# Key-value products of the first block moved behind their chunk's output products, in a linear-attention and mixture-of-experts kernel

## The chip, the cores and the metric

The kernel runs on one core of one Trainium2 chip. The metric is device time in microseconds (us) of one execution, as a median over runs.

## The reference

Three layers follow one another. The first is a linear attention with decay: for each batch and head a state of 48 x 48 is decayed by `w` and gains the outer product of key and value at each of 768 positions; the output at a position is the receptance vector times the state, plus a term of the position itself weighted by `u`. The second is a dense layer pair, the third a mixture of 8 experts, top 2.

```python
for t in range(S):
    kt, vt, rt = (k[:, :, t], v[:, :, t], r[:, :, t])
    cur = np.einsum('bhd,bhe->bhde', u[None] * kt, vt)
    y[:, :, t] = np.einsum('bhd,bhde->bhe', rt, state + cur)
    state = w[None, :, :, None] * state + np.einsum('bhd,bhe->bhde', kt, vt)
...
h = x @ w_in
r = np.maximum(h, 0.0)
g = r * r
return (g @ w_out).astype(np.float32)
```

Sizes: 4 batches, 8 heads, 768 positions, head dimension 48; 3072 tokens of 384; dense width 2048; expert width 1024.

## The kernel before, in words

**Chunks.** The attention is cut into chunks of 128 positions, numbered q = 0 to 23, six to a batch (`CPB`). A chunk with all its heads gives 128 tokens of 384. The steps of a chunk:

- `pre`, `pre_k`, `pre2` (lines 386 to 424): elementwise products of receptance and keys on GpSimd, a reduction on VectorE (line 414), diagonal blocks of the score tile `am` on ScalarE (line 419).
- `p_tr` (line 426): transposes of receptance (`r`) and keys (`k`) on TensorE into one bank each (line 439), then a multiply on VectorE (line 444) or a copy on ScalarE (line 448) out of it.
- `p_a` (line 454): scores, 16 matmuls into two banks (line 459), then two masked copies on VectorE into `am` (line 463).
- `p_y` (line 467): the output in one bank. Part 0 multiplies the state `Z` (24 matmuls, none in the first chunk of a batch), part 1 the scores and values (32 matmuls), all on line 477. Behind part 1 stands `load(q + 2, "v")` (line 491): the values have two buffers, so chunk q + 2 takes that of chunk q.
- `p_kv` (line 494): the key-value product, 32 matmuls into one bank (line 503), then two VectorE operations that take it out into the next state (line 510, or 513 in the first chunk of a batch) and, except in the first chunk, two multiplies on GpSimd (line 511). In the last chunk of a batch it returns at once (line 496).
- `p_x` (line 515): the output is split into a high part on ScalarE (line 522) and a low part on VectorE (line 523), which are the input of the dense layer.

**Banks.** Outside the opening list, `p_tr`, `p_a`, `p_y` and `p_kv` all draw their PSUM bank by `bank()` with the tag "att" (line 171), which has three banks. A bank is given back, in the order of the program, behind the last instruction that uses it.

**Blocks and slots.** The dense layers run over six blocks of 512 tokens (four chunks each). In block j, 16 steps f alternate `mm1` (line 532, nine matmuls into hidden columns, line 540), `gsplit` (ReLU and square, lines 545 to 555), and `mm2` of two steps earlier (line 558, lines 565 and 571). Behind `mm1` of step f stands slot 2f, behind `mm2` slot 2f + 1. Into these slots the table `CHUNKS` (line 36) puts the chunk steps of the next block: one row for each of four chunks, nine times in the order pre, p_tr r, p_tr k, pre2, p_kv, p_a, p_y part 0, p_y part 1, p_x. The whole part of a number is the slot, the fraction the place in it. So in block 0 the chunks 4, 5, 6 and 7 are placed. Chunks 0 to 3, and the first steps of chunk 4, stand in the opening list `HEAD` (line 27).

**Conversion.** In block 0 the dense weights, pieces 0 to 15, are converted beside the matmuls: `conv_w1` (line 270) on ScalarE (line 272), `conv_w2` (line 274) four steps on VectorE (lines 279, 280, 281 and 288 or 291), `conv_w3` (line 294) on ScalarE (line 301) and GpSimd (line 302). Their slots stand in `CONV_AT`. `conv_w2` of piece 5 is in slot 4, that of piece 13 in slot 21.

**Order.** The schedule is by hand: each engine does its instructions in the order in which the program issues them.

Of the kernel before, what the change touches and what calls it, by code (L numbers as in the profile page):

```python
# [34 lines left out]

CHUNKS = (((0.72, 2.09, 0.63, 0.83, 1.23, 3.2, 1.96, 5.12, 6.53),
# [56 lines left out]
def body(ctx, tc, r, k, v, w, u, w_in, w_out, w_gate, w_noise, noise, w1, w2, out):  # L93
# [11 lines left out]
    CPB = S // P  # L105
# [65 lines left out]
    def bank(tag="att", bufs=3):  # L171
        return ps.tile([P, 512], F32, name=tag, tag=tag, bufs=bufs)
# [11 lines left out]
    def load(q, names="rkv"):  # L184
        if q >= NCH:
            return
        b, c = divmod(q, CPB)
        for nm in names:
            if nm in L.get(q, {}):
                continue  # L190
            if nm == "r" and q < QD:
                t = rp[q % 2][:, :, :D]
            elif nm == "r":
                t = at.tile([P, H, D], F32, name="lr", tag="s3", bufs=1)
            elif nm == "k" and q == 0:
                t = kp[0][:, :, :D]
            elif nm == "v":
                t = at.tile([P, H, D], F32, name="lv", bufs=2)
            else:
                t = at.tile([P, H, D], F32, name="l" + nm, bufs=2)  # L200
            nc.sync.dma_start(t, SRC[nm][b, :, c * P:(c + 1) * P, :].rearrange("h s d -> s h d"))
            L.setdefault(q, {})[nm] = t
# [178 lines left out]
                          C["zero2"][:, None, :].to_broadcast([P, b - a, DM]))  # L381

    x1h, x1l = {}, {}
    A = {}

    def pre(q):
        a = A.setdefault(q, {})
        l = L[q]
        if q:
            pre_k(q)  # L390
        if q < QD:
            t = at.tile([P, H, D], F32, name="ra", bufs=2)
        else:
            t = at.tile([P, H, D], F32, name="rk", bufs=1)
        nc.gpsimd.tensor_mul(t, l["r"], l["k"])
        nc.gpsimd.tensor_mul(t, t, ub)
        a["rk"] = t
        load(q + 2, "k")

    def pairs(q):  # L400
        return L[q]["v"].rearrange("p (a s) d -> p a (s d)", s=2)
# [8 lines left out]
    def pre2(q):  # L410
        a, l = A[q], L[q]
        t = a["rk"]
        dg = at.tile([P, H], F32, name="dg", bufs=2)
        nc.vector.tensor_reduce(dg, t, axis=AX.X, op=OP.add)

        a["am"] = at.tile([P, H, P], F32, name="am", tag="am", bufs=2)
        if q < OWN_ACT:
            for h in range(H):
                nc.scalar.activation(a["am"][:, h, :], ident, AF.Copy, scale=dg[:, h:h + 1])
        else:  # L420
            nc.gpsimd.tensor_mul(a["am"], ident[:, None, :].to_broadcast([P, H, P]),
                                 dg[:, :, None].to_broadcast([P, H, P]))

        nc.gpsimd.tensor_copy(ends(q), pairs(q)[:, :, 32:64].rearrange("p a (s x) -> p a s x", s=2))

    def p_tr(q, which, *tag):
        a = A.setdefault(q, {})
        if q >= QD:
            t = a[which + "T"] = at.tile([P, HP, P], F32, name=which + "T", bufs=2)
            nc.vector.transpose(t.rearrange("p a (s i) -> p a i s", i=TQ),  # L430
                                turned[which].rearrange("p a (i x) -> p a i x", x=D)[:, :, :, :32])
            nc.gpsimd.tensor_mul(t[:KR], t[:KR], T[:KR] if which == "r" else T[:KR, :, ::-1])
            if which == "k":
                load_next(q + 1)
            return
        src = (rp if which == "r" else kp)[q % 2]
        pb = bank(*tag)
        for hp in range(HP):
            nc.tensor.transpose(pb[:KR, hp * P:(hp + 1) * P],
                                src.rearrange("p h x -> p (h x)")[:, hp * P:hp * P + KR], ident)  # L440
        t = at.tile([P, HP, P], F32, name=which + "T", bufs=2)
        src = pb[:KR].rearrange("p (h t) -> p h t", t=P)
        if which == "r":
            nc.vector.tensor_mul(t[:KR], src, T[:KR])
        elif q == 0:
            nc.vector.tensor_mul(t[:KR], src, T[:KR, :, ::-1])
        else:
            nc.scalar.activation(t[:KR], src, AF.Copy)
        if which == ("r" if q == TPB else "k"):
            if q + 2 < QD:  # L450
                load(q + 2, "r")
        a[which + "T"] = t

    def p_a(q, *tag):
        a = A[q]
        pbs = [bank(*tag), bank(*tag)]
        for hp in range(HP):
            for j in range(2):
                nc.tensor.matmul(pbs[j][:, hp * P:(hp + 1) * P], a["kT"][64 * j:64 * j + D, hp, :],  # L459
                                 a["rT"][64 * j:64 * j + D, hp, :], start=True, stop=True)  # L460
        am = a["am"].rearrange("p (h j) t -> p h j t", j=2)
        for j in range(2):
            nc.vector.copy_predicated(am[:, :, j, :], mask.bitcast(mybir.dt.uint16)[:, None, :].to_broadcast([P, HP, P]),  # L463
                                      pbs[j].rearrange("p (h t) -> p h t", t=P))

    def p_y(q, part):
        a = A[q]
        c = q % CPB  # L470
        if part == 0:
            a["y"] = bank()
        pb = a["y"][:, :DM].rearrange("p (d t) -> p d t", t=P)

        def add(g, x, y, **kw):
            d, n = divmod(g, 4)
            nc.tensor.matmul(pb[32 * n:32 * n + 32, d, :], x, y, skip_group_check=True, **kw)  # L477

        if part == 0:
            for g in range(KD * 4 if c else 0):  # L480
                hp, s = divmod(g, 3)
                add(g, Z[c % 2][:KR, hp, 32 * s:32 * s + 32], a["rT"][:KR, hp, :], start=(g < 4), stop=False)
            return
        v, am = pairs(q), a["am"].rearrange("p (a s) t -> p a s t", s=2)
        for g in range(KD * 4):
            hp, s = divmod(g, 3)
            add(g, vx[q % 2][:, hp, 0, :] if s == 1 else v[:, hp, 32 * s:32 * s + 32], am[:, hp, s // 2, :],
                start=(g < 4 and c == 0), stop=(s != 1))
        for hp in range(HP):
            add(3 * hp + 1, vx[q % 2][:, hp, 1, :], am[:, hp, 1, :], start=False, stop=True)  # L490
        load(q + 2, "v")


    def p_kv(q, *tag):
        c = q % CPB
        if c == CPB - 1:
            return
        pb = bank(*tag)[:, :HP * D].rearrange("p (a d) -> p a d", d=D)
        kf = kp[q % 2].rearrange("p h x -> p (h x)")
        v = L[q]["v"]  # L500
        for hp in range(HP):
            for g in range(4):
                nc.tensor.matmul(pb[32 * g:32 * g + 32, hp, :], kf[:, hp * P + 32 * g:hp * P + 32 * g + 32],  # L503
                                 v[:, 2 * hp + g // 2, :], start=(hp == 0), stop=(hp == HP - 1), skip_group_check=True)
        for s in range(2):
            rows = slice(64 * s, 64 * s + D)
            zn = Z[(c + 1) % 2][rows, :, s * D:(s + 1) * D]
            w_ = wmid[rows, :, None].to_broadcast([D, HP, D])
            if c:
                nc.vector.tensor_add(zn, pb[rows], Z[c % 2][rows, :, s * D:(s + 1) * D])  # L510
                nc.gpsimd.tensor_mul(zn, zn, w_)
            else:
                nc.vector.tensor_mul(zn, pb[rows], w_)

    def p_x(q, *tag):
        j, i = divmod(q, TPB)
        if i == 0:
            x1h[j] = m1.tile([P, KD, BLK], F32R, name="x1h", bufs=2)
            x1l[j] = m1.tile([P, KD, BLK], F32R, name="x1l", bufs=2)
        src = A[q]["y"][:, :DM].rearrange("p (d t) -> p d t", t=P)  # L520
        hi = x1h[j][:, :, i * P:(i + 1) * P]
        nc.scalar.activation(hi, src, AF.Copy)
        nc.vector.tensor_tensor(x1l[j][:, :, i * P:(i + 1) * P], src, hi.bitcast(F32), op=OP.subtract)
        if q + 1 == QD:
            load_next(QD)
        del A[q], L[q]
# [536 lines left out]
    for j in range(NB):  # L1063
# [6 lines left out]
        if j + 1 < NB:  # L1070
            for i, at_ in enumerate(CHUNKS[min(j, 2)]):
                q = (j + 1) * TPB + i
# [194 lines left out]
```

## Time and profile before

| | us |
|---|---|
| median of 3 runs | 951.79 |
| lowest, highest | 951.40, 951.82 |
| profiled execution | 954.92 |
| span of the profiled execution, first to last instruction | 953.1 |
| busy TensorE in it | 938.8 |

The profile is that of one execution. Its span is what the rows below count in, from 0 to 953.1 us; the remaining 1.8 us lie around it. TensorE's mean granted clock was 0.998 of full speed.

### The profile page before, as it was taken

What the parts mean: (1) busy time and instruction counts of PE and PEld (TensorE: products, weight loads), DVE (VectorE), ACT (ScalarE), POOL (GpSimd) and SP (SyncE); (2) the same over time, 40 slices, a digit from 0 to 9 for tenths busy, and PEclk for the clock granted to TensorE, in tenths of its full rate; (3) what the DMA queues carried; (4) which work ended last, traced back from release to release, by engine and by line L of the source; (5) the groups of instructions that cost most, each with busy time, mean ns of one, the idle gap of its engine ahead of it and who ended that gap; (6) DMA issues with size and microseconds to landing.
All of it is one profiled execution on the core that took longest, in us unless ns stands there. A gap on an engine that the chain in (4) does not pass through costs nothing.

```text
span 953.1 us, 17746 instructions
## 1 busy us (share of the span) xinstructions
PE 938.8 (98%) x6845; PEld 805.3 (84%) x6845; DVE 540.4 (57%) x982; ACT 432.9 (45%) x792; POOL 349.2 (37%) x406
## 2 busy tenths in 40 slices
PE   8899999999999999999999999999999999999997
PEld 7677787778778878877888899999999898989987
DVE  8999756636845663684254564554545555356420
ACT  5666655334434444443555542443444444444321
POOL 6665353544573354455030344122121221212112
PEclk9999999999999999999999999999999999999999
DMA  7655379932432464442024367466545565545212
GB/s 179 165 163 165 96 191 302 244 108 64 94 104 56 111 153 122 111 99 86 1 100 93 108 134 188 104 135 135 130 97 115 120 121 109 114 92 109 36 21 37
DMA packets 193233, 112.32 MB, mean 118 GB/s; under 512 B 131777, under 2 KB 185698, under 8 KB 193122
## 3 DMA queue, kind: packets, MB, share of 16 engines
q1 hardware_dynamic: 181698, 91.03, 37.7%
q0 software_dynamic: 10624, 19.74, 11.3%
q8 instruction: 75, 1.23, 0.5%
q14 instruction: 36, 0.29, 0.1%
q10 hardware_dynamic: 800, 0.02, 0.0%
HBM read 74.64 MB, written 36.12 MB: 116 GB/s over the span
## 4 chain that ended last, share of the span: by engine, by line
PE 90%; DVE 5%; issue 1%; POOL 1%; ACT 1%; DMA 1%; POOLq 0%; DVEq 0%; ACTq 0%
PE ph L540 20%; PE xo L571 19%; PE ph L861 19%; PE y L918 14%; PE y L949 4%; PE att L477 3%; PE ph L949 2%; PE att L459 2%; PE att L604 2%; PE y L861 2%; PE xo L565 1%; PE att L962 1%; PE att L503 1%; DVE am L463 1%; DVE t L279 1%
## 5 line engine op out<-in xcount | busy, mean ns | idle before, releaser
L929 POOL DMA_INDIRECT out<-yt,id x56 | 87.1, 1556 | 298.1 <-ACT yt L927 257.4
L555 DVE TENSOR_TENSOR gl<-g,gh 128x512 fp32r<-128x512 f32 x90 | 77.2, 857 | 127.3 <-ACT gh L553 124.2
L904 DVE SCALAR_TENSOR_TENSOR hl<-ph,hh 128x512 fp32r<-128x512 f32 (+1 forms) x112 | 66.9, 599 | 113.1 <-ACT hh L903 109.2
L545 ACT ACTIVATE rt<-ph 128x512 f32<-128x512 f32 x96 | 57.1, 595 | 150.9 <-PE ph L540 146.4
L540 PE MATMUL ph<-x1h,wih 128*128 128x512 f32 x288 | 119.4, 414 | 0.0
L861 PE MATMUL ph<-xh,w0h 128*128 128x512 f32 (+3 forms) x336 | 118.1, 352 | 0.0
L861 PE MATMUL ph<-xl,w0h 128*128 128x512 f32 (+3 forms) x336 | 116.3, 346 | 0.2 <-DVE xl L830 0.2
L861 PE MATMUL ph<-xh,w0l 128*128 128x512 f32 (+3 forms) x336 | 116.1, 346 | 0.0
L540 PE MATMUL ph<-x1h,wil 128*128 128x512 f32 x288 | 112.4, 390 | 0.0
L540 PE MATMUL ph<-x1l,wih 128*128 128x512 f32 x288 | 112.3, 391 | 0.0
L571 PE MATMUL xo<-gh,wol 128*128 128x512 f32 x270 | 105.9, 392 | 0.0
L903 ACT ACTIVATE hh<-ph 128x512 fp32r<-128x512 f32 (+1 forms) x112 | 58.6, 524 | 88.9 <-PE ph L861 84.0
L918 PE MATMUL y<-w1h,hh 128*128 128x384 f32 x256 | 85.7, 335 | 0.0
L918 PE MATMUL y<-w1l,hh 128*128 128x384 f32 x256 | 85.6, 335 | 0.0
L918 PE MATMUL y<-w1h,hl 128*128 128x384 f32 x256 | 85.6, 334 | 0.0
L732 POOL DMA_INDIRECT sent<-row,si x48 | 50.3, 1049 | 61.4 <-DVE gl L555 45.0
L571 PE MATMUL xo<-gh,woh 128*128 128x512 f32 x180 | 71.6, 398 | 0.0
L571 PE MATMUL xo<-gl,woh 128*128 128x512 f32 x180 | 70.1, 390 | 0.0
L861 PEld LDWEIGHTS ph<-xl,w0h 128*128 128x128 f32 x336 | 63.3, 188 | 8.0 <-DVE xl L830 1.3
L861 PEld LDWEIGHTS ph<-xh,w0l 128*128 128x128 f32 x336 | 63.2, 188 | 7.7
L861 PEld LDWEIGHTS ph<-xh,w0h 128*128 128x128 f32 x336 | 63.3, 188 | 6.9 <-ACT xh L829 0.3
L540 PEld LDWEIGHTS ph<-x1h,wih 128*128 128x128 f32 x288 | 54.0, 188 | 16.4 <-issue 3.7
(234 smaller groups left out, 2145.5 us busy)
## 6 DMA issues: line engine op xcount, KB each, us to landing
ws<-in_moe_w SPq DMA_DIRECT2D x128, 96.0 KB
ws<-in_moe_w SPq DMA_DIRECT2D x32, 384.0 KB
sent<-zero SPq DMA_DIRECT2D x8, 1375.5 KB
G<-sent SPq DMA_DIRECT2D x36, 192.0 KB
stg<-in_moe_w_in SPq DMA_DIRECT2D x8, 768.0 KB
stg<-in_moe_w_out SPq DMA_DIRECT2D x8, 768.0 KB
out<-zero SPq DMA_DIRECT2D x5, 960.0 KB
lv<-in_v SPq DMA_DIRECT2D x24, 192.0 KB
```

Of the source, the lines that this page charges most:

```text
L477: nc.tensor.matmul(pb[32 * n:32 * n + 32, d, :], x, y, skip_group_check=True, **kw)
L540: nc.tensor.matmul(ph, wt[qi][:, d, sl], xt[j][:, d, :], start=(n == 0), stop=(n == 3 * KD - 1))
L545: nc.scalar.activation(rt, ph, AF.Relu)
L555: nc.vector.tensor_tensor(gl, g, gh.bitcast(F32), op=OP.subtract)
L571: nc.tensor.matmul(XO[j][:, d, :], wt[qi][:, fo, sl], gt, start=(f == 0 and n == 0), stop=(f == NF - 1 and n == 2))
L732: st = nc.gpsimd.indirect_dma_start(out=sent, in_=s["row"][:, i, :], in_offset=None, out_offset=bass.IndirectOffsetOnAxis(ap=s["si"][:, i, ...
L861: nc.tensor.matmul(ph[:, c], wt[:, d, sl], xt[:, d, c], start=(m == 0), stop=(m == 3 * KD - 1))
L903: nc.scalar.activation(hh[:, :n], ph, AF.Relu)
L904: nc.vector.scalar_tensor_tensor(hl[:, :n], ph, 0.0, hh[:, :n].bitcast(F32), op0=OP.max, op1=OP.subtract)
L918: nc.tensor.matmul(py, ht[:, sl], wt[:, fo, :], start=(m == 0), stop=(m == 3 * NF2 - 1))
L929: st = nc.gpsimd.indirect_dma_start(out=out, in_=yt, in_offset=None, compute_op=OP.add, out_offset=bass.IndirectOffsetOnAxis(ap=IDX[e, un] ...
L949: nc.tensor.matmul(py[d][:, c], wt[:, fo, sl], ht[:, c], start=(m == 0), stop=(m == 3 * NF2 - 1))
```

## The change

It changes one number in each of the four rows of `CHUNKS` for block 0, the place of `p_kv`: it now stands directly behind `p_y` part 1 of the same chunk. And the load of values into the buffer of chunk q is issued by the later of its two readers, `p_y` part 1 and `p_kv`, by a count of the reads; in the last chunk of a batch there is only the one. In the opening list and in the other blocks `p_kv` stands ahead of `p_y` part 1 as before, so there the load stays where it was.

```diff
-CHUNKS = (((0.72, 2.09, 0.63, 0.83, 1.23, 3.2, 1.96, 5.12, 6.53),
-           (3.99, 6.52, 7.82, 8.89, 12.58, 10.32, 14.31, 14.42, 14.572),
-           (8.79, 15.58, 15.74, 17.5, 17.09, 19.34, 20.21, 22.27, 28.57),
-           (18.59, 17.86, 20.56, 22.96, 28.05, 24.63, 28.23, 28.43, 29.69)),
+CHUNKS = (((0.72, 2.09, 0.63, 0.83, 5.14, 3.2, 1.96, 5.12, 6.53),
+           (3.99, 6.52, 7.82, 8.89, 14.43, 10.32, 14.31, 14.42, 14.572),
+           (8.79, 15.58, 15.74, 17.5, 22.28, 19.34, 20.21, 22.27, 28.57),
+           (18.59, 17.86, 20.56, 22.96, 28.44, 24.63, 28.23, 28.43, 29.69)),
...
-    A = {}
+    A, reads = {}, {}
...
+    def v_read(q):
+        reads[q] = reads.get(q, 0) + 1
+        if reads[q] == 1 + (q % CPB < CPB - 1):
+            load(q + 2, "v")
+
     def p_y(q, part):
...
-        load(q + 2, "v")
+        v_read(q)
...
     def p_kv(q, *tag):
...
                 nc.vector.tensor_mul(zn, pb[rows], w_)
+        v_read(q)
```

## Rows read from the trace of the kernel before

**Rows 1.** The page, part 1: busy time of each engine, share of the span, instructions.

```profile
PE 938.8 (98%) x6845; PEld 805.3 (84%) x6845; DVE 540.4 (57%) x982; ACT 432.9 (45%) x792; POOL 349.2 (37%) x406
```

**Rows 2.** Stretches: us, busy PE, PEld, DVE, ACT, POOL (instructions), PEclk, DMA.

```profile
46.00:53.00 7.00, 6.40 (x56) 4.82 (x55) 6.90 (x6) 4.42 (x8) 6.04 (x4) 1.00 0.36 112
53.00:57.00 4.00, 4.00 (x18) 2.87 (x17) 3.90 (x7) 0.75 (x1) 0.00 (x0) 1.00 0.64 187
...
73.00:120.00 47.00, 47.00 (x348) 33.94 (x349) 39.50 (x52) 31.30 (x58) 20.59 (x16) 1.00 0.43 122
```

**Rows 3.** Waits of PE from 30 us on: total us, times, longest.

```profile
PE att L459 <- DVE Z L510: 1.4, 1, 1.4
```

**Rows 4.** PE in order of time: start, length, line, out<-in, count, idle before it.

```profile
38.97 0.49 PE L459 MATMUL att<-rT,kT 48*128 48x128 f32 x2
40.89 1.13 PE L459 MATMUL att<-rT,kT 48*128 48x128 f32 x14 [1.44 <-DVE Z L510]
...
50.52 0.60 PE L439 MATMUL att<-ident,rp 128*112 128x128 f32 x4
...
53.02 0.60 PE L439 MATMUL att<-ident,kp 128*112 128x128 f32 x4
53.38 0.48 PE L540 MATMUL ph<-x1h,wih 128*128 128x512 f32 x1
```

**Rows 5.** DVE in order of time, 40 to 58 us.

```profile
40.02 0.73 DVE L510 TENSOR_TENSOR Z<-att,Z 48x192 f32<-48x192 f32 x2
40.77 1.47 DVE L279 TENSOR_SCALAR t<-t 128x768 f32<-128x768 f32 x1
...
44.05 1.15 DVE L291 SCALAR_TENSOR_TENSOR t<-stg,t 128x768 int32<-128x768 int32 x1
...
45.84 1.36 DVE L463 COPY_PREDICATED am<-mask,att 128x512 f32<-128x512 uint16 x2
...
53.09 0.55 DVE L279 TENSOR_SCALAR t<-t 128x768 f32<-128x768 f32 x1
...
55.26 0.96 DVE L291 SCALAR_TENSOR_TENSOR t<-stg,t 128x768 int32<-128x768 int32 x1
...
56.73 0.55 DVE L523 TENSOR_TENSOR x1l<-att,x1h 128x384 fp32r<-128x384 f32 x1
```

**Rows 6.** ACT and POOL in order of time, around 40 us.

```profile
39.82 0.88 ACT L272 ACTIVATE t<-stg 128x768 f32<-128x768 f32 x1
...
42.36 2.03 POOL L511 TENSOR_TENSOR Z<-Z,wmid 48x192 f32<-48x192 f32 x2
```

**Rows 7.** PE: first row of the output halves of chunks 5 and 7, and what follows.

```profile
70.38 0.86 PE L477 MATMUL att<-rT,Z 112*32 112x128 f32 x24
...
72.84 0.50 PE L571 MATMUL xo<-gh,woh 128*128 128x512 f32 x1
...
110.58 0.84 PE L477 MATMUL att<-rT,Z 112*32 112x128 f32 x24
...
112.23 0.50 PE L571 MATMUL xo<-gh,woh 128*128 128x512 f32 x1
```

**Rows 8.** PE: key-value products of chunks 6 and 7, and the matmul behind chunk 6's transposes.

```profile
80.62 0.55 PE L503 MATMUL att<-lv,kp 128*32 128x48 f32 x32
...
81.50 0.48 PE L540 MATMUL ph<-x1h,wih 128*128 128x512 f32 x1
...
110.22 0.55 PE L503 MATMUL att<-lv,kp 128*32 128x48 f32 x32
```

**Rows 9.** PE and DVE near 100 us: scores and reduction of chunk 7.

```profile
99.61 1.16 PE L459 MATMUL att<-rT,kT 48*128 48x128 f32 x16
...
100.66 0.55 DVE L414 TENSOR_REDUCE dg<-ra 128x8 f32<-128x384 f32 x1
```

**Rows 10.** PE's last matmul, and a stretch behind it (PEclk third from the end).

```profile
946.04 0.34 PE L918 MATMUL y<-w1l,hh 128*128 128x384 f32 x1
...
948.40:948.60 0.20, 0.00 (x0) 0.00 (x0) 0.00 (x0) 0.00 (x0) 0.20 (x1) 0.52 0.00 0
```

## The prediction, made before the changed kernel was run

> **What bounds the kernel now.** I began with the busy shares of the page: TensorE is busy 98% of the span, no other engine over 57% [rows 1]. So the end is set by TensorE's stream, and a change is worth what it adds to or takes from the gaps and the work of that stream. Then I split the span into stretches: from 73 us to 120 us TensorE works 47.00 of 47.00 us [rows 2]. The gaps lie before 73 us, in the first block, where the weight conversion on VectorE is late. The list of waits names one gap that matters: 1.4 us of the chunk product of line 459 on VectorE's line 510 [rows 3].
>
> The order of time shows which it is. The score product of chunk 4 issues two matmuls at 38.97 us and goes on at 40.89 us, after 1.44 us [rows 4]. What releases it is the pair of adds that takes chunk 4's key-value product out of PSUM, 40.02 to 40.75 us [rows 5]. The score product reads nothing of those adds. It wants their bank: the tag "att" has three banks, chunk 4's output holds one from its first half to the end of `p_x`, the key-value product holds one until the adds, and the score product needs two.
>
> **How far behind VectorE is.** The conversion of piece 5 stands in slot 4, ahead of chunk 4's second output half in slot 5. VectorE ends its last step at 55.26 + 0.96 = 56.22 us [rows 5], while TensorE is through with slot 5 before 50.52 us, where it starts the first transposes of chunk 5 [rows 4]. VectorE's queue is in order, so whatever is put into slot 5 there is done about six us after TensorE passes that slot.
>
> **What the change moves.** Chunk 5 is the last of its batch, and `p_kv` returns at once. Chunk 7's product stays in slot 28 and only swaps with the two output halves beside it; same instructions, no cost. Two products really move: chunk 4's from slot 1 to slot 5, chunk 6's from slot 17 to slot 22, each 32 matmuls on TensorE, two VectorE operations and, for chunk 4, two multiplies on GpSimd (chunk 6 starts a batch and has none). The value load of chunk 6, 8 and 9 on SP moves past these matmuls only. For chunk 6 a weight load stands ahead of it on SP that waits for the end of line 291 at 56.22 us [rows 5], and chunk 4's matmuls are done by then: nothing.
>
> **Chunk 4, early side.** The 1.44 us wait goes, since two banks are free when the score product comes. What is late next is the second output half: it waits for the mask copies of line 463, 45.84 to 47.20 us on VectorE [rows 5]. These hardly move. The adds leave VectorE, but its next step, line 279 at 40.77 us, reads what ScalarE's line 272 finishes at 39.82 + 0.88 = 40.70 us [rows 6], so their 0.73 us were spent in a gap. What moves the copies is GpSimd: its multiplies of line 511 (42.36 to 44.39 us) [rows 6] go elsewhere, and beside them line 291 took 1.15 us against 0.96 us at 55.26 us [rows 5]. With line 281 beside it too I take twice 0.2 us, 0.4 us for all that follows on VectorE. The key-value product put behind the output half costs 110.58 - 110.22 = 0.36 us [rows 7, 8]. Early gain and added work cancel: TensorE comes to the second transposes of chunk 5 at about 53.0 us, as before.
>
> **Chunk 4, late side: the step that decides.** Now count banks in slot 7. Chunk 4's output holds one until line 523, the moved key-value product a second until line 510, the first transposes of chunk 5 a third until line 444. Before, the key-value bank had long been free, and the second transposes started unhindered at 53.02 us [rows 4]. Now there is no fourth bank, and all three releasers stand on VectorE behind the conversion of piece 5. The earliest are the moved adds: 56.22 - 0.4 = 55.8 us, plus 0.73 us, plus 0.14 us from their end to the next matmul (40.75 to 40.89) [rows 4, 5], so 56.7 us. TensorE stands for 3.7 us in place of nothing, and starts 3.65 us later than before. If another bank is taken the wait ends behind lines 444 or 523 instead, later: line 523 would end at 56.73 + 0.55 - 0.4 + 0.73 = 57.6 us [rows 5], 1.1 us behind the adds. I take the adds, which come first in the program, and keep 1.1 us for the upper end. GpSimd's multiplies behind the adds cost nothing: GpSimd is idle from 53 to 57 us [rows 2].
>
> **What is given back.** Chunk 5's output halves take 72.84 - 70.38 = 2.46 us, chunk 7's 112.23 - 110.58 = 1.65 us [rows 7]; the 0.81 us between them is waiting for VectorE's copies, and a TensorE that comes 3.65 us later finds them done: -0.81.
>
> **Chunk 6.** Its product and the transposes behind it take 81.50 - 80.62 = 0.88 us [rows 8]; transposes alone take 53.38 - 53.02 = 0.36 us [rows 4]. Removing it there frees 0.52 us, adding it behind the output costs 0.36 us: -0.16. It has a bank question of its own: the score product of chunk 7 in slot 24 now needs the bank that the moved VectorE pair empties, just ahead of the reduction at 100.66 us [rows 9]. Before, TensorE was there at 99.61 us [rows 9]; delayed by over 2.6 us it comes at 102 us or later, behind 100.66 + 0.73 us. Nothing, but only because of the first wait; its cover gone, it would cost 101.4 - 99.6 = 1.8 us.
>
> **The clock.** The granted clock was at its upper level across the 1.44 us gap in the stream; after the last matmul, which ends at 946.38 us, it was at the lower of its two levels (1.2 of 2.4 GHz) from about 948.4 us, 2.0 us later [rows 10]. A 3.7 us gap is longer than both, so a fall is likelier than not. No row has matmuls at the lower level. Bounds: no loss where the clock holds; where TensorE works at half rate for as long as it stood, half of 3.7, so 1.9 us. I take 1.3 us, nearer the end whose row the gap has passed. The Trainium skill, page "TensorE: Matmul & The Clock Gate", section "Why this matters for your kernels", advises against long idle gaps between bursts of matmuls because the engine goes back to half rate. By that rule the term would be the whole 1.9 us and the time 956.4 us.
>
> **Sum.** +3.65 - 0.81 - 0.16 + 1.3 = +4.0 us. The profiled execution took 954.92 us (span 953.1 us), 3.1 us above the median of 951.79 us; I carry the difference over to the median: 955.8 us. From 120 us on nothing changes, and TensorE has no slack to take the delay back.
>
> **Rivals.**
> 1. Slower, without the clock: the wait as above, the clock held. 951.8 + 2.7 = 954.5 us. For it: the upper level at 1.44 us of idle; against it: the fall at the end. It is part of the forecast's mechanism, 0.27; with a loss of clock 0.53.
> 2. About the same: VectorE is earlier than I think. Piece 4's four conversion steps take from 47.20 to 53.09 us, 5.9 us, beside a GpSimd that is busy for 6.04 of the 7 us from 46 us on [rows 2, 5]; piece 5's take 3.1 us beside an idle one. Were they 2.8 us shorter, the wait at the transposes would be near 1 us, and what is given back would cancel it. But then chunk 7's score product meets its own bank wait of up to 1.8 us, so 951.3 to 953.6 us. Against it: GpSimd's work in that stretch isn't changed. Chance 0.15.
> 3. Faster: the removed 1.44 us counts. Place: TensorE between 39 and 53 us. Price: 1.44 + 0.16 us and 0.3 us of the copies' wait, so 949.9 us. It decides only if the moved adds are done on VectorE before TensorE comes to the second transposes at 53.0 us, 3.5 us earlier than I work out, and if the pair of chunk 6 is done before 99.6 us. Chance 0.05.
>
> That the change does little is in the first two: two of its four products move.
>
> **Numbers.** 0.2% (about what a measurement of this kernel can tell from no change) is 1.9 us, 953.7 us upward. The forecast mechanism (rivals' case 1 in it) has 0.80, nearly all of it slower by more than that. Slower 0.81, same 0.14, faster 0.05. The range goes from 953.0 us (the wait 1.5 us shorter, no clock loss) to 957.8 us (954.5 us, the clock at its 1.9 us and the later bank's 1.1 us, and 0.3 us for a clock that stays down longer); it leaves out most of cases 2 and 3.
>
> **What would show it.** Right: in the list of waits the 1.4 us of line 459 is gone and one of 3 to 5 us of line 439 on line 510 (or 444, 523) stands in its place; the second transposes of chunk 5 start at 56 to 57 us; the granted clock drops to near 0.5 in a stretch between 55 and 62 us; chunk 5's output halves run without a wait; mm1 and later run shifted to the end. Wrong: the transposes start near 53 us; then the bank count or VectorE's place is misread. If the wait is there and the clock stays at 1.00, the time is near 954.5 us. A wait of line 459 at about 100 us would be the chunk 7 term that I set to nothing.

## The result, and the profile after

The kernel after takes 956.84 us (median of 5 runs, 955.65 to 957.52), the kernel before 951.79 us beside it: +5.05 us, ratio 1.0052 with an interval of 1.0037 to 1.0067. That is the forecast side, 1.0 us above the forecast of 955.8 us. The profiled execution of after took 957.52 us (span 955.7 us, mean granted clock 0.995); that of before 954.92 us (0.998).

New line numbers: the output's matmul 482 (was 477), the key-value matmul 508 (503), the adds 515 (510), their form in a batch's first chunk 518 (513), GpSimd's multiplies 516 (511), low part 529 (523), `mm1` 546 (540), `mm2` 571 and 577 (565 and 571). Lines up to 463 are unchanged.

The page's busy times of after; [rows 1] answer to it:

```profile
PE 941.8 (99%) x6845; PEld 809.1 (85%) x6845; DVE 541.4 (57%) x982; ACT 433.3 (45%) x792; POOL 346.4 (36%) x406
```

The same 6845 matmuls take 3.0 us more; the other engines differ by -2.8 to +1.0 us. Added idle time alone would have left TensorE's busy time as it was.

The list of TensorE's waits of after, from 30 us on (us in total, times, longest); [rows 3] answer to it:

```profile
PE att L482 <- ACT wih L301: 2.4, 1, 2.4
PE att L439 <- DVE Z L515: 1.9, 1, 1.9
PE ph L508 <- DVE am L463: 0.4, 1, 0.4
```

The 1.4 us of line 459 is gone. In its place stands the wait that was forecast, line 439 on the adds (now line 515), but at 1.9 us instead of 3.7; and a second one of 2.4 us, which the prediction had not sized. In order of time, TensorE of after (start, length, line, out<-in, count, idle before it); [rows 4] answer:

```profile
39.81 1.16 PE L459 MATMUL att<-rT,kT 48*128 48x128 f32 x16
...
47.64 0.27 PE L482 MATMUL att<-am,lv 128*32 128x128 f32 x1 [2.37 <-ACT wih L301]
...
49.46 1.01 PE L508 MATMUL att<-lv,kp 128*32 128x48 f32 x26
...
55.67 0.40 PE L577 MATMUL xo<-gh,wol 128*128 128x512 f32 x1
58.02 0.62 PE L439 MATMUL att<-ident,kp 128*112 128x128 f32 x4 [1.95 <-DVE Z L515]
...
59.34 0.63 PE L546 MATMUL ph<-x1h,wih 128*128 128x512 f32 x1
...
66.92 1.16 PE L459 MATMUL att<-rT,kT 48*128 48x128 f32 x16
```

And VectorE of after; [rows 5] answer:

```profile
46.81 1.34 DVE L463 COPY_PREDICATED am<-mask,att 128x512 f32<-128x512 uint16 x2
...
56.27 0.96 DVE L291 SCALAR_TENSOR_TENSOR t<-stg,t 128x768 int32<-128x768 int32 x1
57.14 0.73 DVE L515 TENSOR_TENSOR Z<-att,Z 48x192 f32<-48x192 f32 x2
```

The second transposes start 0.15 us after the adds end (57.87 us), and the adds stand directly behind piece 5's conversion: releaser and place are those forecast. The 2.37 us names ScalarE's line 301, which is not the cause: the matmul starts at 47.64 us, in the middle of the pair of mask copies of line 463 that it reads. Of a wait for several semaphores, look at what the instruction reads.

The clock, in stretches of after (us; busy PE, PEld, DVE, ACT, POOL with instructions; PEclk third from the end):

```profile
48.80:52.00 3.20, 3.20 (x55) 2.80 (x45) 3.13 (x3) 1.23 (x2) 3.12 (x4) 0.50 0.45 172
52.30:54.00 1.70, 1.70 (x11) 1.43 (x10) 1.67 (x2) 0.36 (x1) 1.05 (x1) 1.00 0.00 0
...
59.10:62.30 3.20, 3.20 (x9) 2.46 (x8) 2.56 (x3) 1.13 (x3) 1.48 (x1) 0.50 0.92 286
```

TensorE's clock fell to the lower level twice, once behind each wait, and each time TensorE was busy in all of the stretch. A matmul of 512 columns takes 0.63 us there (at 59.34 us); at the upper level, in before, it takes 0.39 us:

```profile
53.70 0.39 PE L540 MATMUL ph<-x1l,wih 128*128 128x512 f32 x1
```

(The 0.48 us of [rows 4] at 53.38 us is the time of the first one behind a group of transposes.) From one start to the next it is 0.43 us against 0.23 us. This is where the 3.0 us of busy time come from. The two falls are not a chance of one profile: all ten executions of after (five here, five in e5 below) have a mean granted clock of 0.995, and the fifteen of before beside e5 have 0.997 to 0.999.

To compare executions I set each against its own first dense matmul, the first of line 546 (540 in before). It starts at 32.70 us in before and at 34.16 us in after; these 1.46 us stem from the start of the program and are taken up at the end of the document. How much later than in the profiled execution of before a step then comes, in us (a minus: earlier), with the labels of the experiments below:

| | chunk 4, output half 2 starts | chunk 5, transposes 2 start | chunk 5, scores end | behind chunk 5's output | chunk 6, scores end | chunk 7, scores end | behind chunk 7's output |
|---|---|---|---|---|---|---|---|
| before: place | 14.03 | 20.32 | 28.73 | 40.14 | 54.79 | 68.07 | 79.53 |
| after | -0.55 | +3.54 | +5.19 | +4.29 | +3.71 | +3.99 | +3.98 |
| e1_chunk4_only | -0.51 | +3.57 | +5.18 | +4.30 | +4.33 | +4.27 | +4.27 |
| e2_chunk6_only | +1.12 | +0.52 | +0.52 | +0.28 | -0.33 | +2.03 | +1.99 |
| e3_conv5_behind | -0.54 | +1.43 | +1.42 | +0.56 | -0.03 | +2.44 | +2.43 |
| e4_filled_waits | -0.58 | +3.58 | +3.59 | +2.72 | +2.13 | +3.50 | +3.48 |
| e5_after_again | -0.69 | +3.39 | +4.98 | +4.11 | +3.53 | +3.81 | +3.80 |
| e6_chunk4_freed | -0.57 | +0.54 | +0.58 | +0.61 | +1.30 | +1.92 | +1.92 |
| e7_early_scores | -2.21 | -1.85 | -0.63 | +0.57 | +2.78 | +3.48 | +3.48 |
| e8_before_again | -0.49 | -0.46 | -0.43 | -0.50 | -0.49 | -0.52 | -0.52 |
| e9_held_bank | +1.04 | +3.35 | +3.34 | +2.48 | +2.47 | +2.44 | +2.44 |
| e10_scalar_out | -0.53 | -0.13 | -0.11 | +0.28 | +0.27 | +0.30 | +0.29 |
| e11_scalar_out_filled | -0.58 | -0.24 | -0.25 | +0.28 | +0.52 | +1.21 | +1.20 |

The row of e8, the kernel before a second time, says how well such a row is known: half a microsecond, and that from the first steps on.

### The profile page after: what moved, and what is told of

Same layout as the page of the kernel before. It is cut to its first block, busy times and chain, and to the rows that moved or that the text cites. A ratio compares the mean times of both kernels' runs of the same rounds, so it can differ in the third digit from the quotient of the medians.

```text
span 955.7 us, 17740 instructions
## 1 busy us (share of the span) xinstructions
PE 941.8 (99%) x6845; PEld 809.1 (85%) x6845; DVE 541.4 (57%) x982; ACT 433.3 (45%) x792; POOL 346.4 (36%) x406
## 3 DMA queue, kind: packets, MB, share of 16 engines
q8 instruction: 75, 1.23, 0.5%
## 4 chain that ended last, share of the span: by engine, by line
PE 91%; DVE 5%; ACT 1%; issue 1%; DMA 1%; POOL 0%; POOLq 0%; ACTq 0%; DVEq 0%
PE ph L546 21%; PE xo L577 19%; PE ph L867 18%; PE y L924 14%; PE y L955 4%; PE att L482 3%; PE att L459 2%; PE att L610 2%; PE ph L955 2%; PE xo L571 2%; PE y L867 2%; DMA ws<-in_moe_w 1%; PE att L968 1%; PE att L508 1%; DVE t L279 1%
```

## The experiments

Times are medians; each ratio is against the kernel before, measured beside it on the same chip. The median of before was 951.8 to 954.9 us from one session to the next, so medians of different sessions aren't subtracted.

| | us | before beside it | ratio (95% interval) |
|---|---|---|---|
| e1_chunk4_only | 958.55 | 954.26 | 1.0043 (1.0030 to 1.0056) |
| e2_chunk6_only | 956.33 | 954.26 | 1.0017 (1.0008 to 1.0026) |
| e3_conv5_behind | 957.17 | 954.26 | 1.0027 (1.0018 to 1.0037) |
| e4_filled_waits | 956.66 | 954.26 | 1.0023 (1.0014 to 1.0033) |
| e5_after_again | 956.69 | 952.31 | 1.0040 (1.0027 to 1.0054) |
| e6_chunk4_freed | 953.74 | 952.31 | 1.0013 (1.0004 to 1.0022) |
| e7_early_scores | 956.34 | 952.31 | 1.0040 (1.0027 to 1.0054) |
| e8_before_again | 951.75 | one run | |
| e9_held_bank | 959.16 | 954.91 | 1.0043 (1.0031 to 1.0056) |
| e10_scalar_out | 955.10 | 954.91 | 1.0004 (0.9995 to 1.0013) |
| e11_scalar_out_filled | 956.15 | 954.91 | 1.0018 (1.0009 to 1.0027) |

**e1_chunk4_only.** Of the four numbers of the change only chunk 4's; rows 2 to 4 of the block stay as before, the load rule is that of after.

```diff
-CHUNKS = (((0.72, 2.09, 0.63, 0.83, 1.23, 3.2, 1.96, 5.12, 6.53),
+CHUNKS = (((0.72, 2.09, 0.63, 0.83, 5.14, 3.2, 1.96, 5.12, 6.53),
```

> Only chunk 4's product is moved; those of chunks 5, 6 and 7 stand where they stood before. Theory (bank wait of chunk 5's second transposes, and the clock): all of the loss is chunk 4's, chunk 6 gave 0.16 us; so 957.0 us, 5.2 us over the kernel before, with a wait of line 439 on the moved adds of about 2 us and the clock at 0.50 for some three us behind it. Rival (the two moved products lose about alike): 954.3 us.

+4.3 us. TensorE in order of time, and two stretches:

```profile
56.28 0.62 PE L439 MATMUL att<-ident,kp 128*112 128x128 f32 x4 [1.93 <-DVE Z L515]
```

```profile
46.80:50.20 3.40, 3.40 (x63) 3.09 (x55) 3.33 (x3) 1.50 (x2) 3.32 (x4) 0.50 0.49 186
...
57.00:60.50 3.50, 3.50 (x10) 2.73 (x9) 2.79 (x4) 1.41 (x2) 1.84 (x1) 0.51 1.01 277
```

The wait, both falls of the clock and the whole loss are there with one number moved. Chunk 4 carries the result; what chunk 6 adds to it is, in the profiles, a gain of 0.3 us (behind chunk 5's output the two rows agree, at +4.30 and +4.29; behind chunk 7's they stand at +4.27 and +3.98).

**e2_chunk6_only.** The other three numbers, chunk 4's back at 1.23.

```diff
-CHUNKS = (((0.72, 2.09, 0.63, 0.83, 5.14, 3.2, 1.96, 5.12, 6.53),
+CHUNKS = (((0.72, 2.09, 0.63, 0.83, 1.23, 3.2, 1.96, 5.12, 6.53),
```

> Chunk 4's product is back in slot 1; chunks 5, 6 and 7 stay moved. Theory: TensorE now comes in time to the scores of chunk 7 (near 100 us), and they wait for the bank that chunk 6's moved VectorE pair empties, up to 1.8 us, less 0.16 us: 953.4 us, with a wait of line 459 on line 518 in the list of waits. Rival (chunk 6's move is free or a gain): 951.6 us and no such wait.

+2.1 us. Its waits of TensorE:

```profile
PE att L459 <- DVE Z L515: 1.7, 1, 1.7
PE att L459 <- DVE Z L518: 1.1, 1, 1.1
```

The first is the old wait of [rows 3]. The second is new: chunk 7's scores wait for the bank that chunk 6's moved pair (line 518) empties. That is the term the prediction set at nothing "only because of the first wait". With the cover taken away it is there: from chunk 6's scores to chunk 7's 2.36 us are lost (-0.33 to +2.03). 1.55 of them are the bank (1.1 us of idle time, and two matmuls that issue ahead of it by themselves), 0.3 the product that now stands behind chunk 6's output, and the other 0.5 the wait of that output for its mask copies, since TensorE now comes there earlier. The step alone is a loss, and in after it costs nothing because chunk 4 has already made TensorE late. In this profile the clock also fell at chunk 4's scores, behind the wait of 1.7 us (granted clock 0.50 from 42.4 to 45.7 us). That is the +1.12 us in its row; 0.5 us of it are left at the second transposes, and 0.3 us behind chunk 5's output. Nine of the ten other executions have a mean granted clock of 0.997 to 0.999, against 0.996 in the profiled one, so the median probably holds no such fall.

**e3_conv5_behind.** After, with piece 5's VectorE conversion moved behind the adds.

```diff
-           (4.07, 4.09, 6.53),
+           (4.07, 5.2, 6.53),
```

> The changed kernel with the four VectorE conversion steps of piece 5 put behind chunk 4's moved adds, in slot 5. Theory (the adds are late because they queue behind that conversion): the adds end about 3.1 us earlier, before TensorE comes to the second transposes of chunk 5; that wait and the clock's fall behind it go, the fall at 48 us stays. 952.3 us, or up to 953.6 us where chunk 7's scores then meet the bank of chunk 6. Rival (another release or the transposes' other input is what they wait for): no change, 956.8 us.

+2.9 us, more than expected. TensorE and VectorE in order of time:

```profile
54.00 0.60 PE L439 MATMUL att<-ident,kp 128*112 128x128 f32 x4
```

```profile
50.61 1.66 DVE L288 SCALAR_TENSOR_TENSOR woh<-stg,t 128x768 int32<-128x768 int32 x1
52.19 0.73 DVE L515 TENSOR_TENSOR Z<-att,Z 48x192 f32<-48x192 f32 x2
```

The adds end at 52.92 us and the transposes start with no idle time before them: the wait at the transposes was set by what stands ahead of the adds in VectorE's queue. They are late all the same, by 1.43 us, since the clock's fall behind the first wait (2.3 us here) is now in the open, where the second wait had hidden it before. Further on, chunk 7's scores wait 1.1 us as in e2.

**e4_filled_waits.** After, with 18 and 30 unread transposes into a bank of the tag "ph", put where TensorE waits.

```diff
+    def fill(n):
+        pw = bank("ph", 2)
+        for _ in range(n):
+            nc.tensor.transpose(pw[:, :P], ident, ident)
...
+            put(5.1, fill, 18)
+            put(7.8, fill, 30)
```

> The changed kernel with transposes that nobody reads, 18 ahead of chunk 4's second output half and 30 ahead of chunk 5's second transposes, into a bank of the dense layer. Theory: the granted clock stays at 1.00 in both places; the second transposes still start when the adds free their bank, so the fall at 48 us had cost nothing and the one at 59 us its 1.7 us: 955.1 us. Rival 1 (both falls count): 953.4 us. Rival 2 (the clock costs nothing here): 956.8 us.

+2.4 us by the medians, +3.5 us in the profile's stretch. The added lines shift the numbers by 5 (444 is the transposes' 439, 520 the adds' 515). TensorE in order of time, and a stretch:

```profile
56.42 0.62 PE L444 MATMUL att<-ident,kp 128*112 128x128 f32 x4 [0.40 <-DVE Z L520]
```

```profile
57.00:63.00 6.00, 6.00 (x23) 3.93 (x22) 5.13 (x8) 4.79 (x7) 1.96 (x3) 1.00 0.64 177
```

The transposes start where they did in after (+3.58 against +3.54), though no fall came ahead of them: the first fall cost after nothing, because the adds set that start. And chunk 5's scores end no later than the transposes (+3.59), where after lost another 1.65 us. That is the price of the second fall. Of these 1.65 us only 0.5 are left at the end (+3.48 against +3.98), since chunk 7's scores, coming earlier, then meet the bank wait of e2, 1.1 us here (0.6 us of it idle time).

**e5_after_again.** After, unchanged.

> The changed kernel itself, beside the kernel before on one chip. Theory: from the first dense matmul to 130 us it loses 4.0 us (second transposes 3.5 us later, 1.7 us of clock behind them, 0.9 us of chunk 5's waits given back, 0.3 us gained at chunk 6), and the whole time differs by the same 4.0 us; what the first result showed beyond that, up to 1.0 us, was the clock at the start of the program, which came up at 11.2 us in place of 6.3 us. Rival: the change costs 5 us, and 1 us of it lies outside this stretch.

+4.4 us, its interval from 2.6 to 5.1 us. TensorE in order of time, and two stretches:

```profile
56.85 0.62 PE L439 MATMUL att<-ident,kp 128*112 128x128 f32 x4 [1.96 <-DVE Z L515]
```

```profile
47.20:50.40 3.20, 3.20 (x62) 2.98 (x63) 3.13 (x3) 1.30 (x3) 3.20 (x3) 0.50 0.58 217
57.40:60.70 3.30, 3.30 (x10) 2.54 (x9) 2.47 (x5) 1.41 (x2) 1.92 (x2) 0.50 1.07 306
```

Wait and both falls repeat, and the sum does too (+3.80). The interval doesn't tell 4 us from 5.

**e6_chunk4_freed.** Chunk 4 alone, piece 5's conversion behind the adds as in e3, and the first wait filled with 18 transposes as in e4.

```diff
+           (4.07, 5.2, 6.53),
...
+            put(5.1, fill, 18)
```

> Only chunk 4's product is moved, the conversion of piece 5 stands behind its adds on VectorE, and 18 transposes that nobody reads fill the wait ahead of chunk 4's second output half. Theory (late adds and the clock are the whole cost of the move): no wait of line 439's kind, granted clock 1.00 from 10 us on, chunk 5's second transposes within 0.5 us of the kernel before, and the whole time within 0.5 us of it. Rival (moving the product costs something by itself, by its place on TensorE or GpSimd): still 1 us or more over the kernel before.

+1.4 us, a miss. At chunk 5 it is nearly as expected: the clock is at 1.00 and the transposes are 0.54 us late, but a wait of 0.6 us on the adds is left. VectorE is then later ahead of chunk 6, where its line 279 waits 2.9 us for ScalarE's line 272, against 1.4 us at that place in before; ScalarE itself waits 2.2 us there for a weight piece, against 0.6 us. Between chunk 5's output and chunk 7's scores 1.3 us are lost.

**e7_early_scores.** An attempt at a faster kernel: with chunk 4's bank wait away, its scores are put earlier, and piece 3's and piece 7's last VectorE steps and pieces 4 and 5 behind what TensorE waits for. Only chunk 4's product is moved.

```diff
+CHUNKS = (((0.72, 2.09, 0.63, 0.83, 5.14, 1.98, 1.96, 5.12, 6.53),
...
+           (3.2, 5.2, 5.45),
+           (4.07, 5.25, 6.53),
...
+           (8.14, 9, 10.4),
...
+    LATE_B = {3: 1.99, 7: 10.33}
...
+                    if fn is conv_w2 and n in LATE_B:
+                        put(at_, fn, n, "a")
+                        put(LATE_B[n], fn, n, "b")
```

> An attempt at a faster kernel from the same reading. Only chunk 4's product is moved; its scores go into slot 1 behind the first output half (three banks are free there), the last conversion step of pieces 3 and 7 goes behind the mask copies of chunks 4 and 5, and the conversions of pieces 4 and 5 behind the moved adds. Theory (the first block waits for VectorE's mask copies): chunk 4's second output half starts about 2 us earlier, no bank wait and no fall of the clock; most of it is lost again at chunk 5's output, so 0.5 to 1.0 us below the kernel before. Rival (VectorE has no order that is better, its sum of work sets the block): no gain, within 0.5 us of the kernel before or above.

+4.0 us. TensorE is 2.2 us ahead at chunk 4's output and still 1.85 us ahead at the second transposes. Its longest waits:

```profile
PE att L508 <- DVE x1l L529: 1.2, 1, 1.2
PE att L482 <- DVE am L463: 1.0, 2, 0.8
PE att L459 <- ACT kT L448: 0.8, 1, 0.8
PE ph L546 <- ACT rt L551: 0.7, 1, 0.7
```

The lead is lost, and more with it, in waits on VectorE and ScalarE further on: what is put behind chunk 4's steps in VectorE's queue is late for the steps that follow. No version here beats the kernel before.

**e8_before_again.** The kernel before again, for one profile.

> The kernel before, for its trace on the same chip. Theory: chunk 5's second transposes 20.3 us behind the first dense matmul as in the trace before, and waits named issue from 150 us on where the whole time is about 954 us, none where it is about 952 us. Rival: its stretch from 33 to 130 us varies by itself by 2 us or more, and the losses of the other runs are read against a moving mark.

951.75 us, span 950.0 us. The profiled execution of before that stands ahead of the prediction has four stalls of some 0.4 us that the trace puts to "issue" (lines 477 and 503, 1.5 us in all); this one has none of them. From the first dense matmul to the last matmul, which starts at 946.04 us there and at 942.75 us here, it is 4.0 us shorter, 3.5 of them after chunk 7: so much do two executions of one kernel differ behind the stretch that the change touches. The expectation on the stalls holds: near 200 and 357 us they stand in every trace of e1 to e4 and e9 to e11, beside which before takes 954.3 or 954.9 us, and in none of after and e5 to e8, beside which it takes 951.8 or 952.3 us. So they don't come from the change.

**e9_held_bank.** Before, with one bank held by something tiny: a transpose into a bank and, behind chunk 4's output in VectorE's queue, a copy of 8 columns out of it.

```diff
+    def hold():
+        pb = bank()
+        nc.tensor.transpose(pb[:, :P], ident, ident)
+        nc.vector.tensor_copy(at.tile([P, 8], F32, name="held"), pb[:, :8])
...
+            put(5.2, hold)
```

> The kernel before, with no product moved; in slot 5 one transpose that nobody needs takes a bank of the tag att, and a VectorE copy of 8 columns, at the same place in its queue as the moved adds would have, empties it. Theory (a bank that is held until VectorE comes to slot 5 is the whole cause): chunk 5's second transposes start some 3.4 us later, the clock falls behind that wait, chunk 5's output gives 0.9 us back: about 4.2 us over the kernel before. Rival (the product's own move, its matmuls or its multiplies, cost the time): within 0.5 us of the kernel before.

+4.25 us. TensorE (line 444 is again the transposes), VectorE, and a stretch:

```profile
56.99 0.62 PE L444 MATMUL att<-ident,kp 128*112 128x128 f32 x4 [2.70 <-DVE held L364]
```

```profile
55.81 0.96 DVE L291 SCALAR_TENSOR_TENSOR t<-stg,t 128x768 int32<-128x768 int32 x1
56.68 0.16 DVE L364 COPY held<-att 128x8 f32<-128x8 f32 x1
```

```profile
57.00:63.00 6.00, 6.00 (x24) 4.03 (x24) 4.57 (x7) 4.90 (x8) 1.85 (x1) 1.00 0.82 234
```

A copy of 0.16 us costs as much as the whole change. What is paid is the place in VectorE's queue, not the length of what stands there, and none of the product's own work. In this execution the clock stayed at its upper level behind 2.7 us of idle time and the stretch lost 2.4 us. The median lost 4.25 us, so other executions must have lost more. That the fall of the clock is the difference is likely, and not shown: the executions of 959.54 and 960.86 us have a mean granted clock of 0.995 against 0.997 in the profiled one (957.31 us), but that of 960.15 us has 0.997 too.

**e10_scalar_out.** Chunk 4's product moved as in e1, but ScalarE copies it out of PSUM, and the adds read that copy.

```diff
+        if q == TPB:
+            kv = at.tile([P, H, D], F32, name="rk", bufs=1)[:, :HP, :]
+            nc.scalar.activation(kv, pb, AF.Copy)
+            pb = kv
```

> Only chunk 4's product is moved, and ScalarE copies it out of its bank; VectorE's adds read the copy from SBUF, at the same place in VectorE's queue as in the changed kernel, and the conversions stay where they were. Theory: the bank is free before the second transposes come; their wait is gone, and what remains is the clock's fall ahead of chunk 4's second output half, now with no later wait to hide it: second transposes 1.5 us late, 0.9 us given back, so 0.3 to 0.8 us over the kernel before. Rival (it is VectorE's adds as such, or their data, that the transposes wait for): 4 us over it.

+0.2 us, no difference that can be measured. TensorE, ScalarE, VectorE, and a stretch:

```profile
53.32 0.60 PE L439 MATMUL att<-ident,kp 128*112 128x128 f32 x4
```

```profile
50.70 0.31 ACT L512 ACTIVATE rk<-att 128x192 f32<-128x192 f32 x1
```

```profile
56.14 0.73 DVE L519 TENSOR_TENSOR Z<-rk,Z 48x192 f32<-48x192 f32 x2
```

```profile
46.00:50.00 4.00, 3.13 (x70) 2.64 (x71) 3.93 (x5) 2.18 (x5) 3.77 (x3) 1.00 0.61 201
```

The adds are as late as ever (56.14 us, behind the same conversion), but the transposes start at 53.32 us with no idle time before them, 0.13 us earlier than in before. The product, its place and the late adds cost nothing that can be measured (the interval goes from -0.5 to +1.2 us); the bank did. The first wait of 2.4 us is there as in after, but against the expectation the clock did not fall behind it in this execution, and so the transposes are not 1.5 us late. The other ten executions have a mean granted clock of 0.996 to 0.997 against 0.998 in this one, so a fall in some of them can't be excluded.

**e11_scalar_out_filled.** e10 with the 18 transposes of e4 in the first wait.

```diff
+            put(5.1, fill, 18)
```

> The same with 18 transposes that nobody reads in the wait ahead of chunk 4's second output half. Theory: clock at 1.00 throughout, second transposes within 0.3 us of the kernel before, the whole time within 0.4 us of it: the move of chunk 4's product costs nothing once bank and clock are kept. Rival (the early gain counts): 1 us or more below the kernel before.

+1.2 us, a miss. Chunk 5 is as expected (transposes 0.24 us early). At chunk 6 VectorE is 1 us later, because ScalarE is, because a weight piece landed later: ahead of chunk 6 ScalarE's line 272 waits 1.75 us for a piece of `moe_w_out`, against 0.61 us in before, 0.77 us in e8 and 0.60 us in e10. Why that piece is late here, and in e6, stays open.

## Why the prediction was right, and where it was off

**The wait behind the bank: right, in place, releaser and size of the delay.** VectorE's gain of 0.4 us is there: lines 281 and 291 of piece 3 take 0.96 us each in after and e5, against 1.15 us each in both executions of before. (That GpSimd's multiplies are what slows them is likely, not shown: line 291 starts at 44.05 us and they end at 44.39 us. Counted from the first dense matmul the mask copies come 0.48 us earlier, but so they do in e8, where nothing was moved.) The transposes start 3.54 us later (forecast 3.65). That the bank is what delays them, and not the product's work, is shown from both sides: e10 frees the bank and leaves the rest, e9 holds a bank and leaves the rest out. The Trainium skill, page "TensorEngine Tiling (Array Packing)", section "PSUM Bottleneck", advises using both ScalarE and VectorE to copy results out of PSUM. These runs agree (+0.2 us in e10 against +4.3 us in e1).

**"TensorE comes to the second transposes of chunk 5 at about 53.0 us, as before": wrong.** In after it was ready 1.4 us later, so it stood 1.95 us there and not 3.7. The step counted what TensorE gains and adds ahead of that place (0.55 and 0.4 us, forecast 0.4 and 0.36), but not what the time that it waits there does to the clock. It had named the wait for the mask copies and not worked out its length: the scores end 2.51 us earlier, the copies only half a microsecond, so 2.4 us of idle time stand at chunk 4's output. The clock fell behind it, and TensorE lost 1.56 us to that (e3 against e10 at the transposes, +1.43 and -0.13). The error cost the forecast nothing, because the adds set the start of the transposes whenever TensorE comes (e4).

**The clock: right in kind, undersized.** Forecast 1.3 us, between 0 and 1.9: a choice between two bounds, with no row for the price of a fall. From the second transposes to the end of chunk 5's scores the loss was 1.65 us. The bound of 1.9 us was half of a 3.7 us stand, and the fall came behind 1.95 us of idle time: the idle time does not size the loss. Without a fall that way takes the same in before, e3, e4, e9 and e10, to 0.04 us; with one, in after, e1 and e5, 1.6 us more. The Trainium skill, page "TensorE: Matmul & The Clock Gate", section "Why this matters for your kernels", asks for no long idle gaps between bursts. By it the clock was to fall behind the forecast 3.7 us. It fell behind some 1.95 us in after, e1 and e5, at a price of 1.65 us in after against the 1.9 that I had worked out, and held behind 2.4 us in e10 and 2.7 us in e9: the runs agree that an idle gap can cost the clock, not that only a long one does. The prediction also said that no row has matmuls at the lower level; the start of the same trace has some, as the last section shows.

**Given back: right.** Chunk 5's output -0.90 (forecast -0.81). Chunk 6's product -0.58 where it was taken away (forecast -0.52) and +0.28 where it was put (forecast +0.36), together -0.30 (forecast -0.16).

**Chunk 7's scores: right.** Nothing in after, and 1.55 us with the cover gone, 1.1 us of it idle time (e2, forecast up to 1.8). In e3 and e4 it takes back part of what those gain, so curing one wait of this change uncovers the next.

**The sum.** 3.54 + 1.65 - 0.90 - 0.30 = 3.99 us, and +3.98 is what the profile shows behind chunk 7's output; forecast 3.98. That the two sums agree so closely is luck: the clock's term came out 0.35 us above its forecast, the other three together 0.34 us below theirs. The median says 5.05 us, with 4.0 inside its interval of 3.5 to 6.4 us, and 4.38 us in e5. Against e8 in place of the first profile of before, the same steps lose 4.5 us, and from the first dense matmul to the last (948.66 us in after) 5.2 us. So 4.0 to 4.5 us have their place in the first block. What the last 0.5 to 1 us is stays open: two executions of before differ by more than that behind chunk 7 (e8).

**Rivals.** Case 1 (clock held) is what e9's profile shows in kind, not after's. Case 2 (VectorE 2.8 us earlier) did not come: the conversion of piece 4 takes some 6 us in after as in before, and that of piece 5 still 3.1 us. Case 3, that the removed 1.44 us counts, needed the adds done before TensorE comes to the transposes. e10 meets the need in another way and is not faster: the 1.44 us is then spent at chunk 4's output, waiting for the mask copies (2.4 us there, as in after).

## What to carry to other kernels

Moving a product later moves the release of its bank too. Count the banks held at each slot, and count each as held until the engine that empties it comes to that copy in its queue, not until the matmul is done. Where that queue is long, let another engine empty the bank. And where a change takes a wait away, ask what is waited for next, for how long, and what that does to TensorE's clock.

## What the runs showed of the hardware that was not expected

**A fall of the clock has a price of its own.** Behind idle times of 1.95 us (after, second wait) and 2.4 us (after, first wait) the granted clock went to 0.50, with the same loss of about 1.6 us each. The stretches at 0.50 shown above are of like length too, 3.2 to 3.5 us, and half of that is about the loss. In e2 it fell behind 1.7 us and in e9 behind 1.6 us, at chunk 4's scores, where the wait for the mask copies then got shorter and hid a good part of it. In e9 1.5 us were lost ahead of chunk 4's second output half, and 0.5 us are left behind it:

```profile
42.20:45.60 3.40, 3.40 (x13) 2.60 (x11) 3.30 (x4) 3.04 (x8) 2.67 (x4) 0.50 0.34 135
```

But behind 2.4 us (e10) and 2.7 us (e9, second wait) it stayed at 1.00. So the length of the idle time alone did not decide it here; what did stays open.

**The start of the program differs by up to 1.9 us.** The first dense matmul starts between 32.25 us (e3) and 34.16 us (after) in these profiles; after a second time (e5) has 33.14 us and before a second time (e8) 33.42 us, so it is not the change. Rows of TensorE in before, then in after:

```profile
1.84 4.10 PE L322 MATMUL att<-ident 128*128 128x128 f32 x18 [1.84 <-POOL ident masks.py:199]
...
7.89 1.25 PE L359 MATMUL xo<-ident 128*128 128x128 f32 x10
```

```profile
9.19 2.24 PE L359 MATMUL xo<-ident 128*128 128x128 f32 x10
```

The same ten transposes take 1.25 us in the one and 2.24 us in the other, and the eighteen ahead of them 0.23 us each in both. The profile's clock column prints 1.00 for that time:

```profile
2.00:4.00 2.00, 2.00 (x10) 2.00 (x11) 1.10 (x3) 0.12 (x1) 1.98 (x9) 1.00 0.54 87
```

By the durations TensorE is at its lower level there, in after until some 11 us: the trace's own clock record begins, at the upper level, at 6.3 us in before and at 11.2 us in after. Ahead of that the column is no evidence; the time of one matmul is. The Trainium skill, page "TensorE: Matmul & The Clock Gate", section "Seeing it yourself", warns that the trace's clock events are not always to be trusted. No run here shows a false event: in before and after the durations change where the record begins. The late rise is not the whole of the difference: in e6 the ten transposes take 1.26 us, and its first dense matmul still starts only at 33.73 us.
